# Storing the scaled outputs of a Fourier-mixing and SoLU kernel one loop step later

## The chip, the cores and the metric

The kernel runs on one core of a Trainium2 chip. The core has five engines that run side by side and wait for each other through semaphores: TensorE (PE in the profile; PEld is its loading of weights), VectorE (DVE), ScalarE (ACT), GpSimd (POOL) and SyncE (SP), which here only issues DMA transfers. Transfers are issued from SP, ACT and POOL, and they are carried out by 16 DMA engines that all of them share. An engine takes its own instructions strictly in the order in which they were written: an instruction that has to wait holds up all that stand behind it on that engine, and this holds for SP's transfers too.

The metric is the device time of one execution in microseconds; lower is better. Three executions of the kernel before took 1436.4, 1439.16 and 1440.36 us.

## The reference

```python
def _attn_ref(x):                                   # x: (8, 3136, 256)
    X = np.fft.fft(np.fft.fft(x, axis=1), axis=2)
    return X.real.astype(np.float32)

def _moe_ref(x, w_in, w_out, g_ln):                 # x: (25088, 256), d_ff = 1024
    h = x @ w_in
    e = np.exp(h - np.max(h, axis=-1, keepdims=True))
    solu = h * (e / (np.sum(e, axis=-1, keepdims=True) + 1e-09))
    mu = np.mean(solu, axis=-1, keepdims=True)
    var = np.mean((solu - mu) ** 2, axis=-1, keepdims=True)
    ln = (solu - mu) / np.sqrt(var + 1e-06) * g_ln
    return (ln @ w_out).astype(np.float32)
```

The output of the first is reshaped to 25088 rows of 256 and goes into the second: the real part of a two-dimensional Fourier transform of each sequence, then a feed-forward block with 1024 hidden features, a SoLU activation and a layer norm.

## The kernel before

**Staging.** The eight sequences are worked on in four pairs. A length of 3136 is 49 times 64, so the transform along the sequence is done in two stages. Stage one (`transform1`, L151) multiplies a folded input `y` by a table `F`; its result `z` goes to a DRAM buffer `zd` (L156, on SP). `turn` (L163, on POOL) reads it back in another order as `g`. Stage two (`transform2`, L174 and L176) multiplies `g` by a table `T`. The transform along the features is folded into the first weight matrix, `Wi`.

**Units and steps.** What follows is done in 100 units, 25 to a pair (`Unit`, L187). A unit is one index k1 of stage two; all but the first unit of each pair yield two blocks of 128 output rows, called signs 0 and 1. One turn of the main loop (L432) is a step. In step i TensorE multiplies unit i by `Wi` (`up`, L200), runs `transform2` of unit i+1, sometimes a part of `transform1` of the next pair (`ahead_pe`), and then, for the unit three steps older (`lag = 3`), the second matrix product (`down`, L284), whose result `ps_o` lies in PSUM. VectorE builds `h` and its maximum (L206, L214), ScalarE the exponential (L225), VectorE the product `u` (L233), GpSimd the negated mean (L235), ScalarE the squares (L242), GpSimd the scale `rs` (L249 to L257).

**How `u` gets to the second product.** `down` needs `u` transposed. VectorE transposes 32 by 32 blocks (`turn_blocks`, L269) into a buffer `v`, and the blocks are then moved between partitions by DMA (`move_blocks`, L278) into `uT`. The moves are made for two units at once: in every second step, when the second unit of the couple is transposed, SP issues 16 transfers of 128 KB each. Such a couple is called a batch below. Its first unit is read by `down` two steps after the moves are issued, its second unit three steps after. `v` and `uT` have two buffers each.

**The outputs.** `store` (L287) is called twice in a step, once for each sign of the old unit. For each it has ScalarE scale `ps_o` by `rs` into a buffer `ot` (L290, four buffers), and then issues the transfer of `ot` to the output: for sign 0 on SP (L296), for sign 1 an indirect transfer on POOL (L293), which takes the rows' places from a table. The call for sign 0 stands ahead of `move_blocks` in the step, so on SP the store L296 of step i stands ahead of the batch's 16 moves of step i. On ScalarE, L290 stands behind the two squares L242 of the same step. The call for sign 1 stands at the end of the step.

**What else is on SP.** The loads of the next pair's input (`xa`, L98, and `x0`, L106) and the stores `zd` (L156). In the pairs 0 and 2 the stores `zd` fall in the steps that have moves, ahead of them; in pair 1 they fall in the steps between. The last pair has no next pair, and on SP only stores and moves.

**What sets the order.** Nothing is scheduled by a planner: each engine runs its instructions as the Python text calls them. The framework adds the semaphores, and picks the buffers of a pool in turn. Each SP transfer also waits until the eighth transfer ahead of it on that queue has landed, since eight semaphores are used in turn.

Of the kernel before, what the change touches and what calls it, by code (L numbers as in the profile page):

```python
# [8 lines left out]
FP32 = mybir.dt.float32  # L9
# [6 lines left out]
P = 128  # L16
# [3 lines left out]
NK = N1 // 2 + 1  # L20
# [4 lines left out]
NC = NH // CH  # L25
# [8 lines left out]
def kernel(  # L34
# [19 lines left out]
    nc = tc.nc  # L54
    B, S, D = x.shape
# [3 lines left out]
    NP = B // 2  # L59
# [4 lines left out]
    out_k = out.rearrange("(p k2 k1) d -> p k1 k2 d", p=NP, k1=N1)  # L64
# [17 lines left out]
    idx = const.tile([P, NP * (NC + NK - 1)], I32, name="idx")  # L82
# [4 lines left out]
    class Pair:  # L87
        def __init__(self, p):
            self.p = p
            self.raw, self.y, self.y0 = {}, {}, None  # L90
            self.g = {}
# [74 lines left out]
    def transform2(pr, k1):  # L166

        i, k = divmod(k1, KG)  # L170
        g = pr.g[i]
        ps = ps_m.tile([P, KD * P + 1], FP32, tag="m", name="ps2")
        for h in range(KD):
            nc.tensor.matmul(ps[:, h * P : (h + 1) * P], g[:, k, h * P : (h + 1) * P], T[:, k1, :],  # L174
                             start=(h == 0), stop=True, skip_group_check=True)
        nc.tensor.matmul(ps[:, KD * P :], T[:, k1, :], g[:, k, P : P + 1],  # L176
                         start=False, stop=True, skip_group_check=True)
        return ps

    def take2(ps):  # L180
        q = qpool.tile([P, KD * P + 1], FP32, tag="q", name="q")
        nc.scalar.copy(q, ps)  # L182
        return q
# [3 lines left out]
    class Unit:  # L187


        def __init__(self, p, k1):  # L190
            self.p, self.k1 = p, k1
            self.signs = (0, 1) if k1 else (0,)
            self.h, self.u = [None] * 2, [None] * 2

    def up(t, c):

        ps = ps_h.tile([P, FF], FP32, tag=f"h{c}", name=f"ps_h{c}")
        for half in range(2):
            fs = slice(half * HW, (half + 1) * HW)
            nc.tensor.matmul(ps[:, fs], t.q[:, c * P : (c + 1) * P], Wi[:, c, fs], start=True, stop=True)  # L200
        return ps

    def even(t, ps):

        t.ev = fpool.tile([P, FF], FP32, tag="ev", name="ev", bufs=1)
        nc.vector.scalar_tensor_tensor(out=t.ev, in0=w_mid, scalar=t.q[:, KD * P :], in1=ps,  # L206
                                       op0=ALU.mult, op1=ALU.add)

    def join(t, ps):

        t.nmax = small.tile([P, 2], FP32, tag="nmax", name="nmax")
        for s in t.signs:
            t.h[s] = fpool.tile([P, FF], FP32, tag="h", name="h", bufs=2)
            nc.vector.tensor_tensor_reduce(out=t.h[s], in0=t.ev, in1=ps, scale=1.0, scalar=-3.0e38,  # L214
                                           op0=ALU.subtract if s else ALU.add, op1=ALU.max,
                                           accum_out=t.nmax[:, s : s + 1])
        n = len(t.signs)
        t.neg = small.tile([P, 2], FP32, tag="neg", name="neg")
        nc.vector.tensor_scalar(out=t.neg[:, 0:n], in0=t.nmax[:, 0:n], scalar1=-1.0, scalar2=None, op0=ALU.mult)  # L219

    def expo(t):
        t.esum = small.tile([P, 2], FP32, tag="esum", name="esum")
        for s in t.signs:
            t.u[s] = fpool.tile([P, FF], FP32, tag="u", name="u", bufs=2)
            nc.scalar.activation(out=t.u[s], in_=t.h[s], func=ACT.Exp, bias=t.neg[:, s : s + 1],  # L225
                                 accum_out=t.esum[:, s : s + 1])

    def product(t, s):

        if s == 0:  # L230
            t.usum = small.tile([P, 2], FP32, tag="usum", name="usum")
            t.nmean = small.tile([P, 2], FP32, tag="nmean", name="nmean")
        nc.vector.scalar_tensor_tensor(out=t.u[s], in0=t.h[s], scalar=1.0, in1=t.u[s], op0=ALU.mult,  # L233
                                       op1=ALU.mult, accum_out=t.usum[:, s : s + 1])
        nc.gpsimd.tensor_scalar(out=t.nmean[:, s : s + 1], in0=t.usum[:, s : s + 1], scalar1=-1.0 / FF,  # L235
                                scalar2=None, op0=ALU.mult)
# [43 lines left out]
    def down(t, s):  # L280
        uT = t.batch.uT[:, t.w].rearrange("p c i (n s) -> p c (i n) s", s=2)
        ps = ps_m.tile([P, D], FP32, tag="m", name="ps_o")
        for c in range(KF):
            nc.tensor.matmul(ps, uT[:, c, :, s], Wo[:, c, :], start=(c == 0), stop=(c == KF - 1))  # L284
        return ps

    def store(t, s, ps):  # L287

        ot = fpool.tile([P, D], FP32, tag="ot", name="ot", bufs=4)
        nc.scalar.mul(out=ot, in_=ps, mul=t.rs[:, s : s + 1])  # L290
        if s:
            i = NP * NC + t.p * (NK - 1) + t.k1 - 1
            dma = nc.gpsimd.indirect_dma_start(  # L293
                out=out, out_offset=bass.IndirectOffsetOnAxis(ap=idx[:, i : i + 1], axis=0), in_=ot, in_offset=None)
        else:
            dma = nc.sync.dma_start(out=out_k[t.p, t.k1], in_=ot)  # L296

        tc.declare_no_dep(dma.ins, group=f"out{1 - s}", reason="other rows of the output")
        tc.add_to_no_dep_group(f"out{s}", dma.ins)

# [89 lines left out]
    def ahead(pr, step):  # L392

        c, r = divmod(step - 2, 2)
        if step == 0:
            load(pr, 0)
            load(pr, 1)
        elif 0 <= c < NC:
            if r == 0:
                add_mirror(pr, c)  # L400
            else:
                fold(pr, c)
                if c + 2 < NC:
                    load(pr, c + 2)

    def ahead_pe(pr, step):

        if 0 <= step - 4 < NH // 2:
            transform1(pr, step - 4)
        elif step - 4 >= NH // 2:  # L410
            turn(pr, step - 4 - NH // 2)

    with tc.manual_schedule():
        pairs = [Pair(p) for p in range(NP)]
        nc.sync.dma_start(out=idx, in_=mirror)
        nc.scalar.dma_start(out=F, in_=f_tab)
        ahead(pairs[0], 0)
        nc.vector.memset(ones, 1.0)
        nc.vector.memset(neg_half, -0.5)
        nc.vector.memset(T, 0.0)  # L420
        with tc.tile_pool(name="prep", bufs=1) as prep:
            prepare = load_weights(prep)
            for step in range(1, NK):
                ahead(pairs[0], step)
                ahead_pe(pairs[0], step)
            prepare()
        fpool = ctx.enter_context(tc.tile_pool(name="fpool", bufs=2))

        units = [Unit(p, k1) for p in range(NP) for k1 in range(NK)]
        units[0].q = take2(transform2(pairs[0], 0))  # L430
        lag = 3
        for i in range(len(units) + lag):  # L432
            cur = units[i] if i < len(units) else None
            nxt = units[i + 1] if i + 1 < len(units) else None
            old = units[i - lag] if i >= lag else None
            ahd = pairs[cur.p + 1] if cur and cur.p + 1 < NP else None
            last = i >= len(units) - 2
            if cur:
                if i % 2 == 0:
                    batch = Batch()  # L440
                cur.batch, cur.w = batch, i % 2
                even(cur, up(cur, 0))
                odd = up(cur, 1)
            if nxt:
                nxt.q = take2(transform2(pairs[nxt.p], nxt.k1))
            if cur:
                join(cur, odd)
                expo(cur)
            if ahd:
                ahead_pe(ahd, cur.k1)  # L450
            if old:
                ps_o = [down(old, s) for s in old.signs]
            if cur:
                for s in cur.signs:
                    product(cur, s)
                for s in cur.signs:
                    square(cur, s)
                    turn_blocks(cur, s)
            if old:
                store(old, 0, ps_o[0])  # L460
            if cur:
                if last:
                    move_blocks(batch, slice(cur.w, cur.w + 1))
                elif cur.w:
                    move_blocks(batch, slice(0, 2))
                stats(cur)
            if ahd:
                ahead(ahd, cur.k1)
            if old and 1 in old.signs:
                store(old, 1, ps_o[1])  # L470


def _tables(B, S, D):
# [73 lines left out]
```

## Time and profile before

| What | Value |
|---|---|
| three executions | 1436.4, 1439.16, 1440.36 us (median 1439.16) |
| the profiled execution | 1439.43 us, of which span 1437.7 us |
| mean granted share of TensorE's clock | 0.923 |
| TensorE busy with matmuls | 1234.3 us, 86% of the span |
| VectorE, ScalarE, GpSimd busy | 960.4, 615.1, 557.0 us |
| chain of work that ended last, by engine | PE 58%, SP queue 15%, DVE 10%, DMA 9% |
| bytes moved by DMA | 189.53 MB, 144.45 MB of them on SP's queue |

The span is the time from the first to the last instruction of the profiled execution; 1.7 us of the execution lie around it. The page divides the span into 40 slices; the first five (some 180 us) prepare the tables and the first pair, and the main loop fills the other 35. Matmul ends are modelled, and so a busy TensorE is not one at its peak. A granted share of 1.00 is TensorE's clock of 2.4 GHz, one of 0.50 is 1.2 GHz. The profile infers from semaphores what ended a wait. `down` waits for the eight semaphores that SP's transfers use in turn, and so the transfer named as the one that ended its wait can be a neighbour of the one it needs.

### The profile page before, as it was taken

Reading aid. Unit: us, or ns where it says so; the run is one execution under the profiler, and the core shown is the slowest. Engines: PE = TensorE matmul, PEld = TensorE weight load, DVE = VectorE, ACT = ScalarE, POOL = GpSimd, SP = SyncE. Lnnn points to the kernel's source line nnn. Section 1 sums busy time; section 2 is a strip of 40 time slices with the busy share of each in tenths; the row PEclk is TensorE's granted clock in tenths of the full one; section 3 lists DMA queues with packets and bytes.
Section 4 is the critical chain, followed back from the end, with each engine's and each line's share of the span. In section 5 each row is a group of like instructions: output and inputs, shape, how many; then the busy total and the mean of one; then the engine's idle time right before and its main releaser. Section 6 shows DMA issues by size and latency. Waiting matters only on the chain.

```text
span 1437.7 us, 15866 instructions
## 1 busy us (share of the span) xinstructions
PE 1234.3 (86%) x4864; PEld 929.4 (65%) x4864; DVE 960.4 (67%) x1481; ACT 615.1 (43%) x1149; POOL 557.0 (39%) x972
## 2 busy tenths in 40 slices
PE   1633599999988899999977999999998898898888
PEld 1412376767766677777755777767676576776667
DVE  2597877667765767777656667767765856675671
ACT  1100445445543545554434355545543544454452
POOL 3430435444343444443344345444442323332331
PEclk9566899999999999999989999999999899999998
DMA  9640497795878758786688597886868557465564
GB/s 246 200 97 0 84 159 153 143 166 114 147 147 149 146 122 162 157 158 118 137 142 162 89 171 140 152 153 123 153 125 140 94 97 120 83 113 101 103 116 89
DMA packets 464628, 189.53 MB, mean 132 GB/s; under 512 B 433206, under 2 KB 446782, under 8 KB 464288
## 3 DMA queue, kind: packets, MB, share of 16 engines
q1 hardware_dynamic: 444752, 144.45, 58.1%
q0 software_dynamic: 13824, 38.55, 9.9%
q10 hardware_dynamic: 5968, 5.52, 1.7%
q8 instruction: 40, 0.66, 0.2%
q14 instruction: 44, 0.36, 0.1%
HBM read 44.78 MB, written 38.80 MB: 58 GB/s over the span
## 4 chain that ended last, share of the span: by engine, by line
PE 58%; SPq 15%; DVE 10%; DMA 9%; ACT 3%; issue 3%; POOL 2%; POOLq 0%; DVEq 0%; ACTq 0%
PE ps_o L284 37%; PE ps_h L200 16%; SPq L278 15%; DMA out_dram<-ot 4%; DMA uT<-v 3%; DVE h L214 2%; PE ps L151 2%; DMA xa<-in_x_dram 2%; DVE ex L312 2%; PE ps L174 2%; ACT h L242 1%; ACT u L225 1%; DVE u L233 1%; POOL nmean L235 1%; DMA xb<-in_x_dram,idx 1%
## 5 line engine op out<-in xcount | busy, mean ns | idle before, releaser
L284 PE MATMUL ps_o<-Wo,uT 128*128 128x256 f32 x3136 | 743.5, 398 | 100.4 <-DMA out_dram<-ot 58.1
L284 PEld LDWEIGHTS ps_o<-Wo,uT 128*128 128x128 f32 x3136 | 641.1, 206 | 181.9 <-issue 107.8
L200 PE MATMUL ps_h<-Wi,q 128*128 128x512 f32 x800 | 363.4, 597 | 7.4 <-DVE ev L206 6.4
L233 DVE SCALAR_TENSOR_TENSOR u<-h,u 128x1024 f32<-128x1024 f32 x196 | 232.5, 1223 | 139.2 <-ACT u L225 139.2
L235 POOL TENSOR_SCALAR nmean<-usum 128x1 f32<-128x1 f32 x196 | 128.7, 657 | 505.1 <-DVE u L233 504.9
L225 ACT ACTIVATE u<-h,neg 128x1024 f32<-128x1024 f32 x196 | 223.5, 1141 | 192.9 <-DVE neg L219 192.9
L242 ACT ACTIVATE h<-u,nmean 128x1024 f32<-128x1024 f32 x196 | 223.8, 1143 | 124.3 <-POOL nmean L235 124.3
L214 DVE CUSTOM_DVE_ANT_0 h<-ev,ps_h 128x1024 f32<-128x1024 f32 x196 | 231.7, 1219 | 50.4 <-PE ps_h L200 49.4
L206 DVE SCALAR_TENSOR_TENSOR ev<-w_mid,q,ps_h 128x1024 f32<-128x1024 f32 x100 | 127.8, 1278 | 202.4 <-PE ps_h L200 202.1
L200 PEld LDWEIGHTS ps_h<-Wi,q 128*128 128x128 f32 x800 | 152.8, 191 | 157.8 <-issue 148.4
L269 DVE STREAM_TRANSPOSE v<-u 128x1024 f32<-128x1024 f32 x200 | 238.5, 1234 | 0.1
L182 ACT COPY q<-ps 128x257 f32<-128x257 f32 x100 | 37.4, 374 | 257.7 <-PE ps L176 254.9
L293 POOL DMA_INDIRECT out_dram<-ot,idx x96 | 103.1, 1074 | 113.1 <-ACT ot L290 91.1
L290 ACT ACTIVATE ot<-ps_o,rs 128x256 f32<-128x256 f32 x196 | 83.6, 460 | 121.1 <-PE ps_o L284 121.1
L151 PE MATMUL ps<-y,F 98*100 98x258 f32 (+3 forms) x288 | 81.7, 424 | 42.4 <-DVE y L113 42.4
L254 POOL TENSOR_SCALAR v<-ssq 128x2 f32<-128x2 f32 (+1 forms) x100 | 27.8, 278 | 169.7 <-ACT h L242 169.7
L174 PEld LDWEIGHTS ps<-T,g 128*128 128x128 f32 x400 | 60.4, 191 | 47.4 <-issue 47.4
L151 PEld LDWEIGHTS ps<-y,F 98*100 98x100 f32 x288 | 48.7, 193 | 56.4 <-DVE y L113 25.5
L120 POOL TENSOR_TENSOR xa<-xa,xb 98x1020 f32<-98x1020 f32 (+1 forms) x32 | 72.8, 2274 | 25.4 <-DMA xa<-in_x_dram 16.7
L257 POOL TENSOR_TENSOR rs<-v,neg_half 128x2 f32<-128x2 f32 (+1 forms) x100 | 72.1, 721 | 7.8
L174 PE MATMUL ps<-T,g 128*128 128x128 f32 x400 | 60.7, 274 | 0.0
L163 POOL DMA_DIRECT2D g<-zd x80 | 47.9, 608 | 20.6 <-DMA zd<-z 11.6
(53 smaller groups left out, 492.9 us busy)
## 6 DMA issues: line engine op xcount, KB each, us to landing
uT<-v SPq DMA_DIRECT2D x784, 128.0 KB
zd<-z SPq DMA_DIRECT2D x32, 400.0 KB
g<-zd POOLq DMA_DIRECT2D x80, 160.0 KB, 5.1
out_dram<-ot SPq DMA_DIRECT2D x100, 128.0 KB
xa<-in_x_dram SPq DMA_DIRECT2D x32, 392.0 KB
raw_in_moe_w_in_dram<-in_moe_w_in_dram ACTq DMA_DIRECT2D x1, 2048.0 KB
raw_in_moe_w_out_dram<-in_moe_w_out_dram ACTq DMA_DIRECT2D x1, 2048.0 KB
uT<-v SPq DMA_DIRECT2D x32, 64.0 KB
```

Of the source, the lines that this page charges most:

```text
L151: nc.tensor.matmul(o[..., cs], F[:, 2 * t + h, :], i[..., cs], start=first, stop=True, skip_group_check=True)
L174: nc.tensor.matmul(ps[:, h * P : (h + 1) * P], g[:, k, h * P : (h + 1) * P], T[:, k1, :], start=(h == 0), stop=True, skip_group_check=True)
L200: nc.tensor.matmul(ps[:, fs], t.q[:, c * P : (c + 1) * P], Wi[:, c, fs], start=True, stop=True)
L206: nc.vector.scalar_tensor_tensor(out=t.ev, in0=w_mid, scalar=t.q[:, KD * P :], in1=ps, op0=ALU.mult, op1=ALU.add)
L214: nc.vector.tensor_tensor_reduce(out=t.h[s], in0=t.ev, in1=ps, scale=1.0, scalar=-3.0e38, op0=ALU.subtract if s else ALU.add, op1=ALU.max, ...
L225: nc.scalar.activation(out=t.u[s], in_=t.h[s], func=ACT.Exp, bias=t.neg[:, s : s + 1], accum_out=t.esum[:, s : s + 1])
L233: nc.vector.scalar_tensor_tensor(out=t.u[s], in0=t.h[s], scalar=1.0, in1=t.u[s], op0=ALU.mult, op1=ALU.mult, accum_out=t.usum[:, s : s + 1])
L235: nc.gpsimd.tensor_scalar(out=t.nmean[:, s : s + 1], in0=t.usum[:, s : s + 1], scalar1=-1.0 / FF, scalar2=None, op0=ALU.mult)
L242: nc.scalar.activation(out=t.h[s], in_=t.u[s], func=ACT.Square, bias=t.nmean[:, s : s + 1], accum_out=t.ssq[:, s : s + 1])
L269: nc.vector.transpose(out=t.batch.v[:, t.w, :, o], in_=t.u[s])
L278: nc.sync.dma_start(out=uT[b, i], in_=v[a, q])
L284: nc.tensor.matmul(ps, uT[:, c, :, s], Wo[:, c, :], start=(c == 0), stop=(c == KF - 1))
```

## The change

`store` is split. `scale` is the old ScalarE instruction, called where `store` was called, so that the scaling stays where it is; its result is kept with the unit, and there are six buffers `ot` in place of four. `store` now only issues the transfers, of both signs, and it is called at the head of the next step, ahead of everything else in it; a last call follows the loop.

```diff
-    def store(t, s, ps):
-
-        ot = fpool.tile([P, D], FP32, tag="ot", name="ot", bufs=4)
-        nc.scalar.mul(out=ot, in_=ps, mul=t.rs[:, s : s + 1])
-        if s:
-            i = NP * NC + t.p * (NK - 1) + t.k1 - 1
-            dma = nc.gpsimd.indirect_dma_start(
-                out=out, out_offset=bass.IndirectOffsetOnAxis(ap=idx[:, i : i + 1], axis=0), in_=ot, in_offset=None)
-        else:
-            dma = nc.sync.dma_start(out=out_k[t.p, t.k1], in_=ot)
...
+    def scale(t, s, ps):
+        t.ot[s] = fpool.tile([P, D], FP32, tag="ot", name="ot", bufs=6)
+        nc.scalar.mul(out=t.ot[s], in_=ps, mul=t.rs[:, s : s + 1])
+
+    def store(t):
+
+        for s in t.signs:
+            if s:
+                i = NP * NC + t.p * (NK - 1) + t.k1 - 1
+                dma = nc.gpsimd.indirect_dma_start(
+                    out=out, out_offset=bass.IndirectOffsetOnAxis(ap=idx[:, i : i + 1], axis=0),
+                    in_=t.ot[s], in_offset=None)
+            else:
+                dma = nc.sync.dma_start(out=out_k[t.p, t.k1], in_=t.ot[s])
...
             last = i >= len(units) - 2
+            if i > lag:
+                store(units[i - lag - 1])
             if cur:
...
             if old:
-                store(old, 0, ps_o[0])
+                scale(old, 0, ps_o[0])
             if cur:
                 if last:
                     move_blocks(batch, slice(cur.w, cur.w + 1))
...
             if old and 1 in old.signs:
-                store(old, 1, ps_o[1])
+                scale(old, 1, ps_o[1])
+        store(units[-1])
```

TensorE, VectorE, ScalarE and GpSimd run the same instructions in the same order as before. On GpSimd this is so because the old call for sign 1 ended a step and the new one opens the next. On SP the order changes.

SP in pair 2, the steps 68 to 71 of the main loop, before. `ot_6182` is the sign 0 output that is scaled in step 69, `uT_6044` the batch that is moved in step 69:

```order
L296 DMA out_0_dram<-ot_6105 128x256
L156 DMA zd_5178<-z_6071 100x1024
L296 DMA out_0_dram<-ot_6182 128x256
L278 DMA uT_6044<-v32_6043 32x16x64 x16
L296 DMA out_0_dram<-ot_6279 128x256
L156 DMA zd_5178<-z_6245 100x1024
L296 DMA out_0_dram<-ot_6356 128x256
L278 DMA uT_6218<-v32_6217 32x16x64 x16
```

The same place in the changed kernel:

```order
L300 DMA out_0_dram<-ot_6105 128x256
L156 DMA zd_5178<-z_6071 100x1024
L278 DMA uT_6044<-v32_6043 32x16x64 x16
L300 DMA out_0_dram<-ot_6182 128x256
L300 DMA out_0_dram<-ot_6279 128x256
L156 DMA zd_5178<-z_6245 100x1024
L278 DMA uT_6218<-v32_6217 32x16x64 x16
L300 DMA out_0_dram<-ot_6356 128x256
```

The output that is scaled in a step with moves (`ot_6182`, `ot_6356`) has changed places with that step's 16 moves; the output of the step between (`ot_6105`, `ot_6279`) keeps its place.

SP in pair 1, where `zd` and the loads `xa` fall in the steps without moves; the rows with a minus are the kernel before, those with a plus the changed one:

```order
 L278 DMA uT<-v_2923 32x16x64 x16
+L300 DMA out_dram<-ot 128x256
 L156 DMA zd<-z 100x1024
-L296 DMA out_dram<-ot 128x256
 L98 DMA xa<-in_x_dram 98x1024
-L296 DMA out_dram<-ot 128x256
+L300 DMA out_dram<-ot 128x256
 L278 DMA uT<-v_3085 32x16x64 x16
```

Here the output of the step with moves stands behind the moves and ahead of `zd`, and the output of the step between stands behind the load `xa`, no longer ahead of it.

## Rows read from the trace of the kernel before

**Rows 1.** The page, busy time of each engine, share of the span, instructions.
```profile
PE 1234.3 (86%) x4864; PEld 929.4 (65%) x4864; DVE 960.4 (67%) x1481; ACT 615.1 (43%) x1149; POOL 557.0 (39%) x972
```

**Rows 2.** TensorE's waits, 180 to 1437 us: total us, times, longest.
```profile
PE ps_o L284 <- DMA out_dram<-ot: 58.1, 16, 9.2
PE ps_o L284 <- DMA uT<-v: 16.0, 5, 5.3
PE ps_o L284 <- issue: 15.8, 6, 6.1
...
PE ps_o L284 <- DMA zd<-z: 1.8, 1, 1.8
```

**Rows 3.** Timeline, last pair: start us, duration us, what, count, [idle before].
```profile
1177.09 2.40 DVE L269 STREAM_TRANSPOSE v<-u 128x1024 f32<-128x1024 f32 x2
1179.56 0.82 ACT L290 ACTIVATE ot<-ps_o,rs 128x256 f32<-128x256 f32 x2
1180.04 0.34 SPq L296 DMA_DIRECT2D out_dram<-ot  x1
1180.48 13.12 SPq L278 DMA_DIRECT2D uT<-v  x16
...
1197.18 10.16 PE L284 MATMUL ps_o<-Wo,uT 128*128 128x256 f32 x32 [3.94 <-DMA uT<-v]
1199.12 2.36 DVE L269 STREAM_TRANSPOSE v<-u 128x1024 f32<-128x1024 f32 x2
1203.92 0.47 ACT L290 ACTIVATE ot<-ps_o,rs 128x256 f32<-128x256 f32 x1 [2.23 <-PE ps_o L284]
1204.87 13.24 SPq L278 DMA_DIRECT2D uT<-v  x16
```

**Rows 4.** Windows, last pair: busy of each engine, granted clock, DMA share, GB/s.
```profile
1180.00:1182.00 2.00, 2.00 (x10) 1.07 (x8) 1.47 (x2) 0.38 (x2) 1.67 (x3) 1.00 0.31 84
...
1184.00:1186.00 2.00, 2.00 (x11) 1.82 (x10) 0.53 (x4) 1.54 (x3) 0.00 (x0) 1.00 0.99 169
...
1198.00:1200.00 2.00, 2.00 (x6) 1.55 (x6) 2.00 (x5) 0.68 (x1) 1.69 (x4) 0.50 0.00 0
...
1204.00:1206.00 2.00, 2.00 (x11) 1.82 (x10) 0.00 (x0) 0.40 (x1) 0.00 (x0) 1.00 0.20 66
```

**Rows 5.** Timeline, the first batch of the kernel, with no output store ahead.
```profile
154.59 2.37 DVE L269 STREAM_TRANSPOSE v<-u 128x1024 f32<-128x1024 f32 x2
157.03 13.02 SPq L278 DMA_DIRECT2D uT<-v  x16
```

**Rows 6.** Timeline of TensorE, the second product of single steps.
```profile
247.15 8.84 PE L284 MATMUL ps_o<-Wo,uT 128*128 128x256 f32 x32 [2.26 <-DMA out_dram<-ot]
...
652.48 7.15 PE L284 MATMUL ps_o<-Wo,uT 128*128 128x256 f32 x32 [1.75 <-DMA zd<-z]
...
701.39 8.84 PE L284 MATMUL ps_o<-Wo,uT 128*128 128x256 f32 x32 [1.75 <-issue]
...
734.48 9.41 PE L284 MATMUL ps_o<-Wo,uT 128*128 128x256 f32 x32 [9.24 <-DMA out_dram<-ot]
...
760.31 7.15 PE L284 MATMUL ps_o<-Wo,uT 128*128 128x256 f32 x32 [1.41 <-DMA out_dram<-ot]
...
941.16 10.17 PE L284 MATMUL ps_o<-Wo,uT 128*128 128x256 f32 x32 [2.48 <-DMA uT<-v]
```

**Rows 7.** Timeline, a batch of pair 1 in a step with `turn`.
```profile
705.45 2.36 DVE L269 STREAM_TRANSPOSE v<-u 128x1024 f32<-128x1024 f32 x2
707.68 1.16 POOL L163 DMA_DIRECT2D g<-zd  x2 [2.06 <-issue]
711.48 0.82 ACT L290 ACTIVATE ot<-ps_o,rs 128x256 f32<-128x256 f32 x2
...
712.39 15.72 SPq L278 DMA_DIRECT2D uT<-v  x16
```

**Rows 8.** The output stores, 182 to 1437 us, from issue to landing.
```profile
DMA to landing us min/median/max: 2.4/3.8/7.9
```

More of the change, by code (lines that the diff above doesn't have):

```diff
@@ L192, in __init__ @@
             self.signs = (0, 1) if k1 else (0,)
-            self.h, self.u = [None] * 2, [None] * 2
+            self.h, self.u, self.ot = [None] * 2, [None] * 2, [None] * 2
     def up(t, c):
@@ L285, in down @@
         return ps
-    def store(t, s, ps):
-        ot = fpool.tile([P, D], FP32, tag="ot", name="ot", bufs=4)
-        nc.scalar.mul(out=ot, in_=ps, mul=t.rs[:, s : s + 1])
-        if s:
-            i = NP * NC + t.p * (NK - 1) + t.k1 - 1
-            dma = nc.gpsimd.indirect_dma_start(
-                out=out, out_offset=bass.IndirectOffsetOnAxis(ap=idx[:, i : i + 1], axis=0), in_=ot, in_offset=None)
-        else:
-            dma = nc.sync.dma_start(out=out_k[t.p, t.k1], in_=ot)
-        tc.declare_no_dep(dma.ins, group=f"out{1 - s}", reason="other rows of the output")
-        tc.add_to_no_dep_group(f"out{s}", dma.ins)
+    def scale(t, s, ps):
[10 more added lines that the diff above has]
+                dma = nc.sync.dma_start(out=out_k[t.p, t.k1], in_=t.ot[s])
+            tc.declare_no_dep(dma.ins, group=f"out{1 - s}", reason="other rows of the output")
+            tc.add_to_no_dep_group(f"out{s}", dma.ins)
     def load_weight(pool, w, o, engine):
```

## The prediction

> **What bounds the kernel now.** I read the page first, then TensorE's waits, then the timeline around one such wait, and last the windows over the same stretch. On the page TensorE is busy for 1234.3 of 1437.7 us [rows 1]. Its waits from 180 us on, which is the main loop, are nearly all ahead of `down` (L284): 58.1 + 16.0 + 15.8 + 1.8 = 91.7 us in 16 + 5 + 6 + 1 = 28 waits [rows 2]. The names of what ended them differ, but `down` reads nothing but `Wo` and `uT`, so each is a wait for the last of a batch's moves; an output store is named where it lands next to them.
>
> The timeline shows one cycle of the last pair [rows 3]. VectorE ends the batch's transposes at 1177.09 + 2.40 = 1179.49. SP could then issue the moves, but ahead of them stands the step's output store, which waits for ScalarE's scaling; that begins at 1179.56, behind the squares. The store is issued at 1180.04, the first move at 1180.48, 0.99 us after the transposes. The moves take 13.12 us to issue, and `down` starts at 1197.18 after 3.94 us of waiting. TensorE did nothing else meanwhile, so the 0.99 us lie on the path. From 1184 on the DMA engines are 0.99 busy, but from 1180 to 1182, when the moves begin, only 0.31 [rows 4]: there is room ahead of the batch, not within it.
>
> The wait has a second price. From 1198 to 1200 the granted clock is 0.50, that is 1.2 GHz, where it was 1.00 before the wait [rows 4]; `down` took 10.16 us [rows 3], and 7.15 us where the clock stayed up [rows 6].
>
> Only every other batch is waited for. In the step that waits, the next batch's transposes are not late (they end at 1199.12 + 2.36 = 1201.48), while TensorE is. That batch's store waits for a scaling that itself waits for the late `down` (1203.92), and its moves start 3.39 us after the transposes, at 1204.87 [rows 3]; still no wait follows, since the earlier one has given it time. I call the waiting batches first and the others second.
>
> **The change part by part.** The ScalarE instructions stay where they are, and so do the POOL transfers: the old call ended a step and the new one opens the next, with nothing of POOL between. I cost both at nothing. On SP the store of a step with moves goes behind the 16 moves, and the store of the other steps is at the head of the next, ready since that step's end. So the moves wait for the transposes alone.
>
> How early they can start shows at the kernel's first batch, which has no store ahead: transposes end at 154.59 + 2.37 = 156.96, the moves start at 157.03, 0.07 us later [rows 5]. A first batch thus starts 0.99 - 0.07 = 0.92 us sooner. The same gap, 0.9 to 1.1 us (2.2 at the very first), stands at 23 more of the 28 waits.
>
> Of the four left, three are second batches that are waited for a little; one is 760.31 with 1.41 us [rows 6]. Their gaps are over 3 us, so these waits (4.1 us together) vanish. But each had shielded the first batch after it by as much, which now waits so much longer. I count them at nothing. The fourth is 734.48 with 9.24 us [rows 6]. There GpSimd's `turn` transfers (707.68) hold up the mean, the squares and so the scaling (711.48); the moves start at 712.39, and the transposes ended at 705.45 + 2.36 = 707.81 [rows 7]: a gap of 4.58 us, of which 4.51 go. But it is the second batch behind the wait of 701.39, which shrinks by 0.92 us and, by the clock (below), its `down` by 8.84 - 7.15 = 1.69 [rows 6]; what the step loses in length, this batch loses in time. So 4.51 - 0.92 - 1.69 = 1.9 us.
>
> Waits: 24 x 0.92 = 22.1, less 0.3 at a wait that was only 0.6 long, plus 1.9, is 23.7 us.
>
> Clock: a wait of 1.75 us left `down` at 7.15 us at 652.48, and at 701.39 the same wait made it 8.84; one of 2.26 made it 8.84, one of 2.48 10.17 [rows 6]. So it decides somewhere near 1.75. Five waits of 1.75 to 2.48 us were followed by a slow `down` and fall to 0.8 to 1.6 us: four at 8.84 - 7.15 = 1.69 and 941.16 at 10.17 - 7.15 = 3.02 give 9.8 us. The waits near 4 us fall to 3 and stay slow. Bounds: nothing, if the clock falls at the shorter waits too; and 9 us more, if the seven of the last pair (10.16 - 7.15 = 3.0 each) come down to the 1.69 of a short one, 7 x 1.3. I take 9.8, since the new waits lie under the one at 652.48.
>
> The sum is 23.7 + 9.8 = 33.5 us. The profiled execution took 1439.43 us, 0.3 over the median of 1439.16, so 1439.4 - 33.5 = 1406 us.
>
> The moved store adds nothing: its 0.34 us on SP [rows 3] now lie where SP waits anyway for the next step, and its data goes out behind the batch. What is late next is the chain from one batch's transposes through 13.12 us of moves to `down`, which still ends about 3 us late in the last pair.
>
> **A rule weighed.** A store alone keeps the DMA engines 0.20 x 2.00 = 0.4 us busy: in the window from 1204 to 1206 the only data are those of the store ahead of the batch [rows 4]. The Trainium skill, page "DMA: Bandwidth & Descriptors", section "Issuing engines are not separate DMA queues", says that all transfers run on the same 16 engines and interleave. By that, the store behind the moves could mix with their tail; what that would give is the third rival. The page's section "Queues, rings and completion order" says that on one issuer's ring descriptors are consumed in order, which would keep it behind. No run here shows yet which.
>
> **The rivals.**
> 1. The clock does not come back: the waits shrink, but every one is still followed by 1.2 GHz. For it: 701.39 was slow after 1.75 us, no longer than 652.48 [rows 6]. Only the waits' 23.7 us are left: 1416 us.
> 2. More comes loose: the long waits' `down` falls from 10.16 to 8.84 (9 us, above), and at 734.48 the moves clear the DMA engines before the next step's `turn` loads arrive, worth up to the rest of its 4.51 us, some 3 to 5. 1406 - 14 = 1392 us. Against it: waits near 3 us remain.
> 3. The store's data mixes with the moves' tail and costs each batch 0.4 of the 0.92 us: 24 x 0.52 = 12.5 us, and the clock hardly returns. 1426 us. Against it: both are on SP's queue, and the moves are issued first.
> 4. It does nothing: the moves start earlier, but the DMA engines end them no sooner. Against it: the 0.31 ahead of the batch [rows 4]. 1439 us.
> 5. Slower: the ring of six `ot`. The store of a step with moves leaves SP only when the moves are issued. ScalarE needs the buffer again three steps later, some 33 us by the 22.0 us between the two transposes, two steps apart, at 1179.49 and 1201.48 [rows 3]. If the landing came later, ScalarE would stand still, with the copy `q` (L182) for the next step's `up` queued behind it, and TensorE behind that. Now: scaling done at about 1180.0, moves until 1192.7, issue within 1 us, landing at worst 7.9 us [rows 8]: 21.6 us. It decides from 33 us on, 11 us away; each us over it would cost one in each of some 49 batches, and 1 us over gives 1439.4 - 33.5 + 49 = 1455 us. In pair 1 the same store also delays `zd` by its issue, which the earlier moves make good.
>
> **How the numbers follow.** Forecast 1406 us: 0.60. Rival 1 (1416): 0.16. Rival 2 (1392): 0.12. Rival 3 (1426): 0.06. Rival 4 (1439): 0.04. Rival 5 (1455): 0.02. The range reaches from 1392 to 1424 and takes in the forecast, rival 1 and most of rival 2. About 0.3%, or 4.3 us, can be told from no change here. Faster by more is the forecast and rivals 1 to 3, 0.94; the same is rival 4, 0.04; slower is rival 5, 0.02.
>
> **What would show it.** In the profile of the changed kernel the first move should follow the transposes by under 0.1 us in every batch; the waits of the last pair should be near 3.0 us instead of 3.94, and still come at every other batch; TensorE's waits from 180 us on should sum to about 68 us; five `down`s that took 8.7 us and more should take 7.15. If the gap is gone and the waits stay as long, the DMA engines were the bound and rival 4 holds. If the waits shrink by half of 0.92, it is rival 3. If ScalarE waits for a landing ahead of the scaling (L289), it is rival 5. I would be wrong most easily on the clock, which is a third of the sum and rests on few rows.

## The result, and the profile after

The changed kernel takes 1402.43 us (median of four executions, 1399.24 to 1404.04), the kernel before 1439.76 us on the same footing. The ratio is 0.9742 with a 95% interval of 0.9718 to 0.9766. The profiled execution took 1403.22 us, of which the span is 1401.4 us. The forecast was 1406.

The page's busy row of the changed kernel, as [rows 1]:

```profile
PE 1219.9 (87%) x4864; PEld 919.1 (66%) x4864; DVE 960.7 (69%) x1481; ACT 614.0 (44%) x1149; POOL 555.8 (40%) x972
```

TensorE does the same 4864 matmuls in 14.4 us less; the other engines work as long as before. TensorE's waits from 180 us on, as [rows 2] (total us, times, longest):

```profile
PE ps_o L284 <- DMA out_dram<-ot: 44.1, 13, 6.4
PE ps_o L284 <- DMA uT<-v: 16.3, 6, 6.2
...
PE ps_o L284 <- issue: 3.2, 4, 2.6
PE ps_o L284 <- DMA xa<-in_x_dram: 2.9, 1, 2.9
```

The sum is 66.5 us, where it was 91.7: 25.2 us less.

The timeline of the last pair, as [rows 3]. In this kernel L289 is the scaling and L300 the output store on SP:

```profile
1149.45 2.38 DVE L269 STREAM_TRANSPOSE v<-u 128x1024 f32<-128x1024 f32 x2
1151.89 13.74 SPq L278 DMA_DIRECT2D uT<-v  x16
1151.94 0.81 ACT L289 ACTIVATE ot<-ps_o,rs 128x256 f32<-128x256 f32 x2
...
1165.74 1.95 SPq L300 DMA_DIRECT2D out_dram<-ot  x2
1168.88 7.15 PE L284 MATMUL ps_o<-Wo,uT 128*128 128x256 f32 x32 [3.28 <-DMA uT<-v]
1171.49 2.40 DVE L269 STREAM_TRANSPOSE v<-u 128x1024 f32<-128x1024 f32 x2
1173.95 13.12 SPq L278 DMA_DIRECT2D uT<-v  x16
```

The transposes end at 1149.45 + 2.38 = 1151.83, and the first move follows 0.06 us later, ahead of the scaling. The store goes out behind the sixteen moves, at 1165.74. The second batch starts as promptly (1173.95 after 1173.89). Over 47 batches, the second to the 48th, the mean gap between transposes and first move is 0.06 us, where it was 2.02 us. The batch itself takes about as long as before: its 16 moves are issued within 13.83 us on average, where it was 13.71. Only the last two units, which are moved one by one, still wait after their transposes, 3.55 and 4.17 us (4.26 and 5.53 before).

TensorE's second product of single steps, as [rows 6]:

```profile
495.62 10.13 PE L284 MATMUL ps_o<-Wo,uT 128*128 128x256 f32 x32 [2.57 <-issue]
...
718.54 9.60 PE L284 MATMUL ps_o<-Wo,uT 128*128 128x256 f32 x32 [6.41 <-DMA out_dram<-ot]
...
822.26 8.84 PE L284 MATMUL ps_o<-Wo,uT 128*128 128x256 f32 x32 [2.88 <-DMA xa<-in_x_dram]
...
922.89 7.15 PE L284 MATMUL ps_o<-Wo,uT 128*128 128x256 f32 x32 [1.92 <-DMA uT<-v]
...
1216.07 10.01 PE L284 MATMUL ps_o<-Wo,uT 128*128 128x256 f32 x32 [3.00 <-DMA out_dram<-ot]
```

The page's group of all `down`s, first of the kernel before, then of the changed one (busy us, mean ns of one, idle before):

```profile
L284 PE MATMUL ps_o<-Wo,uT 128*128 128x256 f32 x3136 | 743.5, 398 | 100.4 <-DMA out_dram<-ot 58.1
```

```profile
L284 PE MATMUL ps_o<-Wo,uT 128*128 128x256 f32 x3136 | 730.3, 393 | 75.3 <-DMA out_dram<-ot 44.1
```

So the books are: 25.2 us less of waiting and 743.5 - 730.3 = 13.2 us less of `down`. Against it, the first `down` of the kernel starts 2.3 us later (175.13, where it was 172.84). That makes 36.1 us; the two profiled executions lie 1439.43 - 1403.22 = 36.2 us apart.

### The profile page after: what moved, and what is told of

Its sections match the earlier page's. It is cut to its first block, busy times and chain, and to the rows that moved or that the text cites. A ratio compares the mean times of both kernels' runs of the same rounds, so it can differ in the third digit from the quotient of the medians.

```text
span 1401.4 us, 15865 instructions
## 1 busy us (share of the span) xinstructions
PE 1219.9 (87%) x4864; PEld 919.1 (66%) x4864; DVE 960.7 (69%) x1481; ACT 614.0 (44%) x1149; POOL 555.8 (40%) x972
## 4 chain that ended last, share of the span: by engine, by line
PE 64%; SPq 14%; DMA 9%; DVE 9%; issue 2%; ACT 1%; POOL 1%; POOLq 0%; DVEq 0%; ACTq 0%
PE ps_o L284 42%; PE ps_h L200 17%; SPq L278 13%; DMA out_dram<-ot 3%; DMA uT<-v 3%; DMA xa<-in_x_dram 2%; PE ps L151 2%; PE ps L174 2%; DVE ex L316 2%; DVE h L214 1%; DMA xb<-in_x_dram,idx 1%; DVE u L233 1%; ACT u L225 1%; POOL xa L120 1%; DVE v L269 1%
## 5 line engine op out<-in xcount | busy, mean ns | idle before, releaser
L284 PE MATMUL ps_o<-Wo,uT 128*128 128x256 f32 x3136 | 730.3, 393 | 75.3 <-DMA out_dram<-ot 44.1
L284 PEld LDWEIGHTS ps_o<-Wo,uT 128*128 128x128 f32 x3136 | 631.9, 203 | 153.1 <-issue 80.1
L289 ACT ACTIVATE ot<-ps_o,rs 128x256 f32<-128x256 f32 x196 | 82.9, 459 | 92.1 <-PE ps_o L284 89.1
L163 POOL DMA_DIRECT2D g<-zd x80 | 47.9, 608 | 18.7 <-DMA zd<-z 11.3
```

## The experiments

Theory: SP's wait for the scaling and the issue behind it, ahead of a batch's moves, cost 0.92 us a batch and all that hangs on it; the data of the store cost nothing as long as it goes out behind the batch. The rivals are the six buffers, the store's data, and ScalarE.

### The six buffers alone

```diff
-        ot = fpool.tile([P, D], FP32, tag="ot", name="ot", bufs=4)
+        ot = fpool.tile([P, D], FP32, tag="ot", name="ot", bufs=6)
```

This is the kernel before with six `ot`.

> The kernel before with one number changed: six output buffers in place of four, the stores where they were. Theory (the moves no longer wait for the step's scaling and store; the buffers only make room for that): no difference from the kernel before, 1436 to 1443 us, TensorE's waits ahead of the second product near 92 us. Rival (the scaling had been held up by the ring of four buffers): it would get most of the changed kernel's gain, 1400 to 1410 us.

Measured: 1442.37 us (median of 10, 1423.76 to 1445.12), ratio 1.0012 with an interval of 0.9963 to 1.0062. The waits ahead of `down` are 42.0 + 23.0 + 20.0 + 3.7 = 88.7 us. The buffers alone do nothing that shows.

### The store behind the moves, and nothing else

```diff
             if old:
-                store(old, 0, ps_o[0])
+                ot0 = scale(old, 0, ps_o[0])
...
                     move_blocks(batch, slice(cur.w, cur.w + 1))
...
+            if old:
+                send(old, 0, ot0)
```

The kernel before with its four `ot`. `scale` is the ScalarE instruction, `send` the transfer; the store of sign 0 is issued in its own step, directly behind the moves. Sign 1 stays as it was.

> The kernel before with four buffers, where the sign 0 store is issued on the sync queue directly behind the moves of its own step, not a step later; the sign 1 store stays where it was. Theory: the moves follow the transposes by under 0.1 us as in the changed kernel, and all of the gain is there: 1398 to 1408 us. Rival (what counts is that the stores of the steps between, or the loads that stood behind them, go out at another time): in the steps between nothing changes here, so part of the gain would be missing, 1410 to 1440 us.

Measured: 1400.71 us (1397.46 to 1409.38), ratio 0.9749, 0.9662 to 0.9836. The timeline of the last pair (the store is L299 here):

```profile
1147.73 2.41 DVE L269 STREAM_TRANSPOSE v<-u 128x1024 f32<-128x1024 f32 x2
1150.21 13.96 SPq L278 DMA_DIRECT2D uT<-v  x16
...
1164.27 1.90 SPq L299 DMA_DIRECT2D out_dram<-ot  x2
```

The moves follow the transposes (1150.14) by 0.07 us, and the waits ahead of `down` are 67.2 us, near the 66.5 of the changed kernel. As far as the interval tells, all of the gain is in the one exchange of places on SP. A store "one step later", with the sign 1 transfers moved along, is not needed for it.

### The wait without the data

```diff
+                if old and (last or cur.w):
+                    mark = dram.tile([1, D // 4], FP32, tag="mark", name="mark")
+                    nc.sync.dma_start(out=mark, in_=old.ot[0][0:1, 0 : D // 4])
                 if last:
                     move_blocks(batch, slice(cur.w, cur.w + 1))
```

The changed kernel; ahead of a batch's moves SP sends 256 bytes of the freshly scaled `ot` to a scratch buffer. That transfer waits for the scaling as the old store did, while the store itself, with its 128 KB, stays behind the moves.

> The changed kernel with a transfer of 256 bytes ahead of the 16 moves, which reads the output just scaled and writes it to a scratch place: the wait for the scaling and one issue stand ahead of the moves again, but next to no data; the real store stays where the change put it. Theory (the wait is what cost): the gap from the transposes to the first move is back at 0.9 to 1.0 us, and the time is near that of the kernel before, 1430 to 1442 us. Rival (what cost were the store's 128 KB on the shared DMA engines ahead of the moves): the data is still gone, only the issue of some 0.4 us is added, and the time stays at 1402 to 1414 us.

Measured: 1435.87 us (median of 10, 1431.61 to 1442.88); against the kernel before the ratio is 0.9983, 0.9946 to 1.002. The timeline, first of a batch in which ScalarE is late, then of one in the last pair as [rows 3]:

```profile
1147.15 2.37 DVE L269 STREAM_TRANSPOSE v<-u 128x1024 f32<-128x1024 f32 x2
...
1152.90 0.24 SPq L470 DMA_DIRECT2D mark<-ot  x1
1153.25 13.16 SPq L278 DMA_DIRECT2D uT<-v  x16
...
1176.71 2.41 DVE L269 STREAM_TRANSPOSE v<-u 128x1024 f32<-128x1024 f32 x2
1179.19 0.81 ACT L289 ACTIVATE ot<-ps_o,rs 128x256 f32<-128x256 f32 x2
1179.67 0.24 SPq L470 DMA_DIRECT2D mark<-ot  x1
1180.01 13.75 SPq L278 DMA_DIRECT2D uT<-v  x16
```

With 256 bytes in the old place the gap is back (1180.01 - 1179.12 = 0.89 us; 3.73 us at the late one), and the waits ahead of `down` are 63.7 + 23.2 + 3.2 + 2.7 = 92.8 us. The whole gain is gone. It was the old place that cost, and not the data. Of the 0.89 us, 0.55 are the wait for the scaling (1179.12 to 1179.67), and 0.34 lie from the issue of the short transfer to the first move; the two were not tested apart.

### The store from ScalarE

```diff
-            dma = nc.sync.dma_start(out=out_k[t.p, t.k1], in_=ot)
+            dma = nc.scalar.dma_start(out=out_k[t.p, t.k1], in_=ot)
```

The kernel before; the sign 0 store is issued by the engine that scales, and SP has no output store.

> The kernel before, where the sign 0 store is issued from ScalarE, directly behind its scaling, and is gone from the sync queue. Its 128 KB thus go out at the old time, beside the first moves, but the moves wait for the transposes alone. Theory: the gap falls under 0.1 us and nearly all of the gain is there; the store's 0.4 us of DMA time now lie among the moves, 24 times at most, and ScalarE spends an issue more in each step: 1400 to 1414 us. Rival (the store's data ahead of the moves is what cost): no gain beyond a few us, 1428 to 1440 us.

Measured: 1514.82 us (1510.18 to 1515.57), ratio 1.0518, 1.0432 to 1.0604: neither expectation, and slower than every other kernel here. The gap did go. The timeline (its x19 takes in three moves of the next batch), and one piece of SP's alone:

```profile
1243.80 2.37 DVE L269 STREAM_TRANSPOSE v<-u 128x1024 f32<-128x1024 f32 x2
1246.23 28.88 SPq L278 DMA_DIRECT2D uT<-v  x19
...
1262.30 0.34 ACTq L296 DMA_DIRECT2D out_dram<-ot  x1
...
1267.51 7.15 PE L284 MATMUL ps_o<-Wo,uT 128*128 128x256 f32 x32 [2.98 <-issue]
```

```profile
1264.03 0.59 SPq L278 DMA_DIRECT2D uT<-v  x1
```

The first move follows the transposes by 0.06 us, but the batch's last move is issued from 1264.03 to 1264.62, so that the batch is issued within 18.4 us, where the changed kernel takes 13.1 to 13.8 us in this pair. SP's own waits say why (total us, times, longest; the changed kernel has no such row), and the windows show the DMA engines (DMA share and GB/s last in the row) well over half idle while the last move waits:

```profile
SPq L278 <- DMA out_dram<-ot: 278.1, 58, 9.7
```

```profile
1260.00:1262.00 2.00, 2.00 (x7) 1.09 (x6) 1.73 (x2) 2.00 (x5) 0.20 (x2) 1.00 0.40 61
1262.00:1264.00 2.00, 2.00 (x7) 0.96 (x6) 1.28 (x1) 0.74 (x2) 1.51 (x4) 1.00 0.21 70
```

The moves wait 278.1 us for output stores to land. In the program the eight semaphores are dealt out in turn to the transfers of SP and of ScalarE together. So a move can get the semaphore that a store issued on ScalarE holds, and that store leaves in the next step: here at 1262.30, and the last move, which has the same semaphore in the trace, at 1264.03. One in-order wait was exchanged for another.

### The store from GpSimd

```diff
-            dma = nc.sync.dma_start(out=out_k[t.p, t.k1], in_=ot)
+            dma = nc.gpsimd.dma_start(out=out_k[t.p, t.k1], in_=ot)
-
-        tc.declare_no_dep(dma.ins, group=f"out{1 - s}", reason="other rows of the output")
-        tc.add_to_no_dep_group(f"out{s}", dma.ins)
```

The same question with a queue whose stores take no semaphore from SP's moves. Both signs are now on GpSimd, and as the lines that declared their rows independent are gone, each store there also waits for the landing of the one before it. The wait for the scaling has moved to GpSimd with the store.

> The kernel before, with the sign-0 store issued from GpSimd at its old place in the program; nothing is issued on sync between the transposes and the block moves, and the transfers of sync share their semaphores with each other only. Theory (the 0.92 us ahead of the moves is the whole price, and the ScalarE variant lost by moves that waited for a semaphore lent to a later store): the first move is issued less than 0.1 us after the transposes, a batch of moves ends about 13.1 to 13.8 us after its first, the waits ahead of down in pairs 0 to 11 sum to 60 to 75 us, and the time is 1398 to 1415 us. Rival (it is the store's data beside the moves that costs): the gap is gone as well, but batches end later, the waits stay above 85 us and the time is 1428 us or more.

Measured: 1422.98 us (1419.96 to 1425.26), ratio 0.988, 0.9824 to 0.9935. That lies between the two expectations: some 15 of the 36 us. The timeline of one batch of the last pair:

```profile
1186.43 2.38 DVE L269 STREAM_TRANSPOSE v<-u 128x1024 f32<-128x1024 f32 x2
1188.87 13.53 SPq L278 DMA_DIRECT2D uT<-v  x16
1189.90 0.63 POOL L296 DMA_DIRECT2D out_dram<-ot  x1 [3.09 <-ACT ot L290]
```

The gap is 0.06 us, but the store now goes out 1 us into the batch, and its data with the moves'. In the last pair eight batches (units 80 to 95) are issued within 13.82 us on average, in the changed kernel within 13.36; in six batches of pair 1 (units 30 to 41) it is 13.76 and 13.20. So a store beside the moves costs a batch about 0.5 us, half of what the missing gap gives, and the waits from 180 us on sum to 77.4 us, between 91.7 and 66.5. The late sign 1 store runs beside the moves too, and its share in the 0.5 us wasn't separated. Not all that is missing lies at the moves: from the end of the last matmul to the end of the span this kernel takes 11.3 us (1410.3 to 1421.6), the changed one 4.6 (1396.8 to 1401.4), so some 6.7 us of the 20 between them are lost at the very end, where only outputs are left. And no batch is drawn out by semaphores, which fits the reading of the ScalarE variant.

By the Trainium skill, page "DMA: Bandwidth & Descriptors", section "Issuing engines are not separate DMA queues", all transfers interleave on the same 16 engines, whichever engine starts them. The longer batches of this kernel agree, with about 0.5 us each.

### The changed kernel with four buffers

```diff
-        t.ot[s] = fpool.tile([P, D], FP32, tag="ot", name="ot", bufs=6)
+        t.ot[s] = fpool.tile([P, D], FP32, tag="ot", name="ot", bufs=4)
```

> The changed kernel with four output buffers in place of six. Theory: the store of a step with moves leaves the queue some 14 us after its scaling and lands 3.9 us later, and the buffer is wanted again two steps (22 us) later, so ScalarE hardly ever waits for it: 1398 to 1412 us, and most of the gain does not need the six buffers. Rival (the ring decides): ScalarE waits for landings ahead of the scaling in each step with moves, and the time goes up to 1420 us or more.

Measured: 1398.69 us (1392.87 to 1401.23), ratio to before 0.9732, 0.969 to 0.9775: as fast as with six. Four buffers are enough, though the store of a step with moves leaves some 14 us after the scaling (1151.94 and 1165.74, above). In the changed kernel, with six, only one of ScalarE's waits ahead of a scaling is put down to a landing:

```profile
ACT ot L289 <- DMA uT<-v: 3.0, 1, 3.0
```

It ends at 831.14, where the step's `down` ends too (822.26 + 8.84 = 831.10, in the rows above), and so it is rather a wait for that. With four buffers no landing is named at all.

### A step of slack for the batch

```diff
-        lag = 3
+        lag = 4
```

`down` and all behind it work on the unit four steps older, once in the changed kernel and once in the kernel before. `v` and `uT` keep two buffers each.

> The changed kernel with a lag of four steps in place of three between a unit's first and second product, so that each batch has some 11 us more from its transposes to its reader. Theory (all waits ahead of the second product are the latency of the moves, and the fallen clock follows from the waits): the 66 us of waits and the some 28 us that the second products lose at 1.2 GHz go, and the time is 1300 to 1325 us. Rival (the DMA engines' throughput or the queue is the bound, not the latency): the waits come back at another place and the time stays over 1370 us.

> The kernel before with a lag of four. Theory: where the batch has 11 us to spare, the 0.9 to 4.6 us that the store costs it are hidden, and the time is within 0.5% of that of the changed kernel with a lag of four, 1300 to 1330 us: the change is then worth nothing. Rival (the store's place costs something besides the batch's latency): it stays 20 us or more behind the changed kernel with a lag of four.

Measured: 1301.55 us with the change (1299.82 to 1302.32; ratio to before 0.9062, 0.903 to 0.9094), and 1302.82 us without it (1300.88 to 1304.22; 0.9077, 0.9045 to 0.9109). TensorE's only wait ahead of `down` from 180 us on, with the change:

```profile
PE ps_o L284 <- DMA uT<-v: 2.7, 1, 2.7
```

and without it:

```profile
PE ps_o L284 <- issue: 2.8, 1, 2.8
PE ps_o L284 <- DMA uT<-v: 1.6, 1, 1.6
```

The main loop in one window each (granted clock, DMA share and GB/s last), first of the changed kernel, then of the same with four steps:

```profile
180.00:1390.00 1210.00, 1139.43 (x4650) 870.67 (x4649) 839.97 (x1220) 580.41 (x1093) 499.07 (x893) 0.97 0.75 138
```

```profile
180.00:1290.00 1110.00, 1106.64 (x4654) 854.66 (x4655) 839.18 (x1220) 576.86 (x1092) 500.38 (x895) 1.00 0.82 150
```

With one more step between moves and `down` the waits and the loss of clock are gone, and TensorE is busy in 1106.64 of 1110 us. In the kernel before with four steps the gap is still there:

```profile
1086.99 2.42 DVE L269 STREAM_TRANSPOSE v<-u 128x1024 f32<-128x1024 f32 x2
...
1090.38 13.56 SPq L278 DMA_DIRECT2D uT<-v  x16
```

It is 1090.38 - 1089.41 = 0.97 us, and costs nothing that shows: the two kernels lie within 0.1%. The gap cost something only while the batch ended last. With four steps either kernel is over 9% faster than the kernel before, and over 7% faster than the changed one.

## Why the prediction was right

**The cause.** Right. What stood ahead of the moves, the wait with its issue, was the price (the 256-byte transfer brings all of it back), and the exchange on SP the whole cure. The gap fell below 0.1 us, as said, in every batch of two units.

**The waits, 23.7 us.** Measured 25.2. The term of 0.92 us for each first batch shows in the last pair: 3.28 and 3.00 us where 3.94 and 3.92 were, and still at every other batch. In the first pair it shows only in the sum: there the waits went over to the batches between (units 4, 8 and 12 in place of 2, 6 and 14; up to unit 14 they sum to 3.6 us, where it was 7.8). The three second batches that were waited for wait no more, and pass it on as said: behind 760.31 with its 1.41 us, the next first batch waits 6.21, where it was 6.07. At 734.48 the sum had 9.24 - 1.9 = 7.3 us left; 718.54 has 6.41.

**The clock, 9.8 us.** This step was mis-sized, and its rule is wrong. The five `down`s that it named did fall to 7.15 us and gave 9.7 us, but their waits did not fall to 0.8 to 1.6 us: two are gone, and three are 0.16, 1.17 and 1.92 us. And the rule behind them, that the clock decides near 1.75 us of wait, does not hold. Two waits of the kernel before spoke against it already, longer than 1.75 us and followed by 7.15:

```profile
197.10 7.15 PE L284 MATMUL ps_o<-Wo,uT 128*128 128x256 f32 x32 [2.28 <-DMA out_dram<-ot]
...
839.84 7.15 PE L284 MATMUL ps_o<-Wo,uT 128*128 128x256 f32 x32 [2.40 <-DMA uT<-v]
```

In the changed kernel, in the rows above, a wait of 1.92 us left `down` at 7.15, and so did one of 3.28 (1168.88), while 2.57 made it 10.13 and 2.88 made it 8.84. The windows behind two of the waits, of 3.28 and of 3.00 us, show the granted clock in the third column from the end:

```profile
1170.00:1172.00 2.00, 2.00 (x11) 1.80 (x11) 2.00 (x5) 0.54 (x3) 1.40 (x3) 1.00 0.00 0
1218.00:1220.00 2.00, 2.00 (x6) 1.60 (x5) 2.00 (x3) 0.85 (x1) 1.71 (x4) 0.50 0.00 0
```

The longer wait was followed by 2.4 GHz and the shorter by 1.2 GHz. So steps that the sum left alone moved as well, some to slow (822.26: 8.84 us, where its fellow at 839.84 took 7.15) and more to fast (1168.88: 10.16 before), and these net another 4.8 us; the `down` of the very first unit took 1.3 us longer. Hence 13.2 us for 9.8. Part of this is chance: the kernel before with six buffers runs the same order as the kernel before, and its profiled execution has 735.7 us of `down`, where that had 743.5. Over three kernels with the wait (before, six buffers, 256 bytes) the mean is 739.6 us, over three without it (changed, store behind the moves, four buffers) 730.3: 9.3 us. As a mean, the 9.8 were about right; for this pair of executions they were 3.4 short. That the mean comes so near is luck, since the rule that gave it is wrong. (The bound of 9 us more counted seven slow `down`s in the last pair; the trace has six.)

**The start of the loop.** Not in the sum: the first `down` came 2.3 us later. The code ahead of it is the same in the seven kernels here that keep `lag = 3` and don't issue stores from ScalarE, and their first `down` starts anywhere from 172.8 to 175.3 us. So this is scatter of the staging, and it took back 2.3 of the 3.4 us that the clock gave above the forecast.

**The rivals.** Rival 1 fell: five `down`s came back to 7.15. Rival 2 was half right: more clock came loose, but waits near 3 us stayed, and 734.48 gave 2.8 us and not the whole of its gap. Rival 3 fell for this change: the waits shrank by 25.2 us and not by 12.5, with moves and store on one queue and the moves first. Its price of 0.4 us was near what a store beside the moves does cost (0.5 us, with GpSimd issuing). Rival 4 fell with the waits. Rival 5 was far off, as said: even four buffers do.

## What to carry to other kernels

Where an engine issues transfers in order, look for the instruction that waits ahead of the transfers that the bottleneck needs. An early issue of something nobody waits for costs its whole wait there, and the cure is to put it behind them on the same queue; on another queue its data went out beside the others' (GpSimd: 15 of the 36 us, with some 7 lost at the end) or it shared semaphores with them (ScalarE: 5% slower). And before shaving a chain that ends last by a microsecond, see whether a step more of distance takes it off the path: here that was worth 134 us to the kernel before and 101 us to the changed one.

## What was not expected of the hardware and the program

- The clock after a wait is not set by the length of that wait: 3.28 us kept 2.4 GHz, 1.75 us (701.39, [rows 6]) lost it. What else decides stays open; one profile of a kernel can differ from another of the same order by 8 us in `down` alone (743.5 and 735.7).
- A store on another engine's queue can hold up SP's moves, by a semaphore that both share: 278.1 us of waits in 58 places, with the DMA engines 0.21 to 0.40 busy in the middle of a batch.
- A store of 128 KB that goes out beside a batch of moves lengthens the batch by about 0.5 us. Whether its data goes out ahead of the batch or behind it makes no difference that could be measured: 1435.87 us with 256 bytes ahead and the store behind, 1436.57 us with the store ahead.
